# Moving the second attention projection of one group, and splitting the LayerNorm of its two tiles, in a fused attention + MLP kernel

## The chip, the cores and the metric

The kernel runs on one core of one Trainium2 chip. A core has a matrix engine (PE, with PEld for its weight loads), a vector engine (DVE), a scalar engine (ACT), a general engine (POOL), a queue engine that only issues transfers (SP), and 16 DMA engines. Each engine works through its own instructions in the order in which the program lists them, and waits when one of them needs something that is not there yet. The metric is the device time of one execution in microseconds (us), lower is better.

## What is computed

A pre-norm transformer block on 2048 tokens of width 576, in bfloat16:

```
h  = x + Attention(LayerNorm(x), wqkv) @ wo        # 32 heads of 18
       # token s attends to tokens s, s-2, s-4, ... s-14  (8 keys, softmax)
h2 = h + gelu(LayerNorm(h) @ w1 + b1) @ w2 + b2    # inner width 4608
```

## The kernel before

**Tiles.** The tokens are cut into 16 tiles of 128; tile j holds tokens j, j+16, j+32 and so on, one per partition. So the 8 keys of a tile's tokens lie in tiles of the same parity, and two rings in SBUF (`kv_ring`, one for even tiles and one for odd ones, 8 slots each for keys and values) hold all that a tile needs. Where the window wraps around, the slot must hold the tile shifted down by one partition: `store_halo` writes a tile's keys and values to DRAM, and `halo(j, 1)` (keys) or `halo(j, 2)` (values) reads them back shifted, as soon as the tile itself has been used.

**Stages.** First come the LayerNorm of x and the products with `wqkv` (about 5 to 69 us of the profile). Then the tiles go in pairs, `GROUPS[0]` to `GROUPS[7]`: (14, 12), (10, 8), (6, 4), (2, 0), (15, 13), ... For each pair k a loop body emits MLP1 (`h @ w1` and gelu, 36 row blocks of 128) and MLP2 (`@ w2`). Groups 0 and 1 do MLP2 with 36 rows of matmuls per tile (`mlp2`, line 576); groups 2 to 7 use `mlp2_fast` (line 661), a scheme that needs fewer products of 2x2 blocks but wants sums and differences of the weights (`w2_sums`, line 631) and of the activations (`h_sums`, line 641) from DVE.

**What is threaded between the matmuls.** While group k is in its MLP, the other engines prepare the groups behind it. In the loop body, c and d are the two tiles of group k+1, and e and f those of group k+2. In the round k = 0 that this document is most about, c = 10, d = 8, e = 6, f = 4.

- Attention of a tile, on DVE: `att_qk_a` (line 345, keys times query), `att_qk_rest` (lines 351, 358, 360, then the maximum, 364 and 365), then `att_exp` on ACT (line 383), then `att_den` (391 to 393) and `att_pv_a`, `att_pv_b` (397, 403, 404), which leave the output of attention in `q_all`.
- Its transposition: `dma_out` writes it to a DRAM buffer `td` (lines 193, 194) and a transposing DMA reads it back as `oT` (line 199 or 433), all from SP.
- Projection with `wo`, on PE: `wo_visit` or `wo_duo` (line 217, tile `pw`).
- LayerNorm 2: `ln2_h` (DVE, 461) adds x; `ln2_act` (ACT, 478 to 480) takes mean and variance; POOL raises the variance to the power -1/2 (481); `ln2_send` (ACT, 486 and 177) normalises and sends the tile to `td`; `ln2_ins` has the transposing DMAs that read it back as `hnT` (496), the right operand of MLP1, and two accumulating DMAs from POOL (505) behind them. Both halves of `hnT` are needed before MLP1 of that group begins. `put_b2` (SP, 502) overwrites the tile's x with the bias b2.

**What sets the order.** The order is written by hand: the whole kernel stands in a block in which every engine keeps the program's order. The lists `m1[v]` run ahead of visit v of MLP1 (four visits), `mid[v]` between its phases, and `ia[f]` and `ib[f]` ahead of row f of MLP2 of the group's first and second tile. `late_wo` is a projection that is slipped into the last visit of MLP1. A `wo_visit` with `fill=True` runs two rows of MLP2 between its two halves. ACT changes between two function tables, one with exp and one with gelu; `exps` is an exp followed by `gelu_table`, a one-element gelu that brings the second table back. `after` and `between` are the lists of the qkv stage, by visit: `after[n]` runs behind visit n, `between[n]` behind the first output of visit n.

Of the kernel before, what the change touches and what calls it, by code (L numbers as in the profile page):

```python
# [17 lines left out]
def kernel(  # L18
# [12 lines left out]
    nc = tc.nc  # L31
# [71 lines left out]
    def load(out, in_):  # L103
        ins = nc.sync.dma_start(out=out, in_=in_).ins
        if pace[0] is not None:
            tc.add_manual_dep(ins, pace[0].name, sync_dep, reason="pace of the weight loads")

    def load_x(js):
        j0, n, step = js[0], len(js), 2
        load(x_all[:, j0:j0 + step * (n - 1) + 1:step, :], x3[:, j0:j0 + step * (n - 1) + 1:step, :])  # L110

    def load_wqkv(t, k0=0, k1=KF):
        load(wq_sb[:, k0:k1, t * D:(t + 1) * D],
             A_wqkv[k0 * P:k1 * P, t * D:(t + 1) * D].rearrange("(k p) c -> p k c", p=P))

    def load_wqkv_half(engines, ts):
        src = A_wqkv[KF * P:D, :].rearrange("p (t g c) -> p t g c", t=3, g=2)
        for r in range(2):
            engines[r].dma_start(out=wqh_sb[half_rows(r), ts, :], in_=src[:, ts, r, :])
# [87 lines left out]
    def half_rows(r):  # L207
        return slice(r * HP, (r + 1) * HP)
# [121 lines left out]
    def logit_of(js):  # L330
        home, i = side[js[0]]
        return (x_all[:, 13:16:2, 0:2 * W * H].bitcast(F32).rearrange("p i (w h) -> p i w h", w=W)
                if home else logits[:])[:, i:i + len(js)]

    def sides(js):
        i = side[js[0]][1]
        return slice(i, i + len(js))

    def halo(j, t):
        if j >= 2:  # L340
            ring = (None, k_ring, v_ring)[t]
            nc.sync.dma_start(out=ring[j % 2][:, j // 2, :], in_=kv_dram[j, 0:P, t - 1, :])
# [46 lines left out]
    def att_den(*js):  # L389
        n, sl, lg = len(js), sides(js), logit_of(js)  # L390
        nc.vector.tensor_reduce(out=den[:, sl], in_=lg.rearrange("p i w h -> p i h w"), axis=AX.X, op=ALU.add)  # L391
        nc.vector.reciprocal(out=den[:, sl], in_=den[:, sl])
        nc.vector.tensor_tensor(out=probs[:, sl], in0=lg, in1=den[:, sl].unsqueeze(2).to_broadcast([P, n, W, H]), op=ALU.mult)
# [12 lines left out]
    def att_pv_sum(j):  # L406
        att_pv_a(j)
        att_pv_b(j)
# [264 lines left out]
    def c_(fn, *a):  # L673
        return lambda: fn(*a)
# [71 lines left out]
    with tc.manual_schedule(engines={ENG.PE, ENG.Activation, ENG.DVE, ENG.SP, ENG.Pool}):  # L746
# [1 line left out]
        load_x(EVEN[1:2])  # L748
        load_wqkv(1, 0, 2)
        load_wqkv(1, 2, KF)  # L750
        load_wqkv_half((nc.scalar, nc.scalar), slice(1, 3))
        load_x(EVEN[2:3])
        load_x(EVEN[3:4])
        load_wqkv(2, 0, 2)
        load_wqkv(2, 2, KF)
        load_x(EVEN[4:6])
        load_x(EVEN[6:8])
        load_x(ODD[0:4])
# [75 lines left out]
        A = ATT_ORDER  # L834
# [15 lines left out]
        def ln2_stats(c, d):  # L850
            for j in (c, d):
                ln2_h(j)
                ln2_act(j)
            for j in (c, d):
                put_b2(j)
# [5 lines left out]
                for j in (c, d):  # L861
                    accumulate_h(j)

        def ln2_pair(c, d, js=()):
            ln2_stats(c, d)
            if js:
                att_den(*js)
                att_pv_sum(js[0])
            ln2_send(c)
            ln2_send(d)  # L870
            ln2_ins(c, d)
            if js:
                halo(js[0], 2)

        loads = {v: [c_(load_w1, c)] for c, v in enumerate((3, 4, 9, 14, 16, 18))}
        for n, v in enumerate((20, 21, 22, 23)):
# [3 lines left out]
            1: [c_(ln1_even_rstd, 2, 3), c_(ln1_even, 5)],  # L880
            2: [c_(ln1_even, 6), c_(ln1_even, 7), c_(ln1_even_rstd, 4, 5)],
            3: [c_(ln1_even_rstd, 6, 7), c_(ln1_stats, 8)],
            4: [c_(ln1_rstd, 8), c_(ln1_stats, 9, c_(ln1_bias, 8)), c_(ln1_act, 8, 0), c_(ln1_stats, 10)],
            5: [c_(ln1_act, 8, 1), c_(out_x, 0), c_(ln1_rstd, 9), c_(ln1_bias, 9), c_(att_qk_a, A[0])],
            6: [c_(ln1_rstd, 10), c_(ln1_act, 8, 2), c_(halo, A[0], 1)],
            7: [c_(att_qk_rest, A[0], 0), c_(ln1_bias, 10), c_(ln1_act, 8, 3), c_(in_x, 0), c_(out_x, 1)],
# [12 lines left out]
            20: [c_(ln2_rstd, A[1]), c_(add_b2, A[1]), c_(ln2_bias, A[1]), c_(att_qk_rest, A[2], 0, 1)],  # L899
        }  # L900
        between = {
            10: [c_(att_exp, A[0])],
            13: [c_(att_exp, A[1])],
            18: {1: [c_(tr_o, A[1], "D")]},
# [55 lines left out]
        def wo_visit(*duos, fill=False):  # L960
            visit([wo_duo(j, tag) for j, tag in duos], (lambda: [ahead[0]() for _ in range(2)]) if fill else None)
# [5 lines left out]
        for k, g in enumerate(GROUPS):  # L967
            c, d = GROUPS[k + 1] if k + 1 < len(GROUPS) else (None, None)
            e, f = GROUPS[k + 2] if k + 2 < len(GROUPS) else (None, None)
            m1, mid, ia, ib, late_wo = {0: []}, {}, {}, {}, None  # L970
            if k in (1, 2):
                m1[0].append(c_(finish_out, GROUPS[k - 1][1]))
            if k == 0:
                m1[0] += [c_(halos, 1), c_(att_qk_a, d), c_(att_qk_rest, d, 1), c_(halo, d, 1)]
                mid[0] = {1: [c_(exps, d)]}
                m1[1] = [c_(pv_t, c), c_(pv_t, d), c_(load_w2, 4), c_(att_qk, e, 0)]
                late_wo = wo_duo(c, "B")
                ia[12] = [c_(exps, e), lambda d=d: wo_visit((d, "A"), fill=True), c_(ln2_pair, c, d, (e,)), c_(halos, 2), c_(send_o, e)]
                ib[0] = [c_(finish_out, g[0])]
                ib[4] = [c_(att_qk, f, 1)]  # L980
                ib[8] = [c_(read_o, e)]
                ib[32] = [c_(exps, f)]
            elif k == 1:
                m1[0].append(c_(pv_t, d))
                m1[1] = [c_(att_qk_a, e), c_(halo, e, 1), c_(att_qk_b, e, 0), c_(halos, 7)]
                m1[3] = [c_(att_qk_a, f), c_(halo, f, 1), c_(att_qk_add, f, ((0, 0, 9), (0, 0, 4)))]
                ia[0] = [c_(wo_visit, (c, "B"), (d, "C")), c_(ln2_pair, c, d), c_(att_qk_b, f, 1, 2), c_(att_max, (e, f)),
                         c_(exps, e, f), c_(att_qk_one, GROUPS[4][0], 0, 1), c_(att_den, e, f)]
                ia[2] = [c_(pv_sum, e), c_(dma_tr_o, e), c_(reload_x, GROUPS[4])]
                ib[0] = [c_(finish_out, g[0])]  # L990
            if k < 2:
                mlp1(g, mlp1_plan(p, q, r, s, (s, r, p) if k else (r, s, p)), m1, mid, late_wo)
                mlp2_tile(g, 0, "D", ia)
                mlp2_tile(g, 1, "C", ib)
                continue
            rows = ROWS[k]
            home = k % 2
            x = {n: [] for n in ("h", "6", "7", "in", "exp", "4", "3")}
            if k < 6:
                m1[0] += [c_(pv_sum, d), c_(send_o, d), c_(read_o, d)]  # L1000
                m1[1] = [c_(att_qk_one, f, 1, home ^ 1), c_(att_max, (e, f))]
                m1[3] = []
                if k in (2, 3):
                    m1[3] += [c_(w2_sums, *((0, 8) if k == 2 else (8, 12)))]
                early = {2: (), 3: (0,)}.get(k, (0, 2))
                m1[3] += [c_(h_sums, 0, rows, early)]
                x["h"] += [c_(h_sums, 0, rows, [t for t in range(4) if t not in early])]
                x["exp"] += [c_(exps, e, f), c_(att_den, e, f)]
                x["4"] += [c_(att_pv_a, e), c_(halo, e, 2)]
                x["3"] += [c_(att_pv_b, e), c_(send_o, e), c_(read_o, e)]  # L1010
            else:
                if k == 6:
                    m1[0] += [c_(pv_sum, d), c_(send_o, d), c_(read_o, d)]
                    m1[1] = [c_(w2_sums, *m) for m in ((12, 14), (14, 16), (16, NM))]
                m1[3] = [c_(h_sums, 0, SR)]
                mid[3] = {1: [c_(h_sums, SR, 16)]}
                x["h"] += [c_(h_sums, 16, NM)]
            if k + 3 < len(GROUPS):
                x["7"] += [c_(att_qk_one, GROUPS[k + 3][0], 0, home)]
                x["in"] += [c_(reload_x, GROUPS[k + 3])]  # L1020
            wo = None
            if c is not None:
                if k == 6:
                    x["h"] = [c_(ln2_h, c), c_(ln2_act, c), c_(ln2_h, d)] + x["h"] \
                        + [c_(ln2_more, d), c_(ln2_rstd, d), c_(ln2_send, c), c_(add_b2, c), c_(add_b2, d), c_(ln2_bias, d)]
                    x["6"] += [c_(ln2_hn, d), c_(ln2_out, d)]
                else:
                    x["h"] = [c_(ln2_stats, c, d)] + x["h"]
                    x["6"] += [c_(ln2_send, c)]
                    x["7"] = [c_(ln2_send, d)] + x["7"]  # L1030
                x["in"] = [c_(ln2_ins, c, d)] + x["in"]
                wo = lambda tags: wo_visit((c, tags[0]), (d, tags[1]))
            mlp1(g, mlp1_plan(p, q, r, s, (r, s, p)), m1, mid)
            mlp2_fast(g, rows, (p, q, r, s), wo, x)
            p, q, r, s = r, s, p, q
# [30 lines left out]
```

## Time and profile before

| | us |
|---|---|
| median of 6 runs | 368.08 (367.01 to 369.2) |
| the profiled execution | 368.53 |
| its span, first to last instruction | 366.6 |
| PE busy / DVE busy / ACT busy / POOL busy in the span | 358.7 / 299.7 / 231.8 / 40.9 |
| qkv stage ends, MLP1 of group 0 begins | about 69 |
| MLP2 of group 0 begins | 87.6 |
| MLP1 of group 1 begins | 108.1 |
| MLP2 of group 1 begins | 128.1 |
| MLP1 / MLP2 of group 2 begin | 145.8 / 163.6 |
| MLP1 / MLP2 of group 3 begin | 184.2 / 202.0 |

The profile is of one execution, and all moments in it count from the first instruction. A row of a timeline gives the start, the time, the engine, the source line, the operation, the output and inputs, how many instructions are merged in the row, and in brackets the idle time ahead of it with what ended it. A row of the waits gives who waited, for what, the total, how often, and the longest. In rows of SP the time is that of issuing; a transfer lands later. The granted clock of PE was 0.999 of the full one over the span.

### The profile page before, as it was taken

To read this page: it belongs to the slowest core of one execution; us is meant where nothing else is said; L and a number is where in the kernel's file an instruction comes from. 1 tells how busy PE (TensorE), PEld (TensorE's weight loads), DVE (VectorE), ACT (ScalarE), POOL (GpSimd) and SP (SyncE) were. 2 spreads that over 40 slices of the span, in tenths; PEclk is the share of its full clock that TensorE was granted. 3 is DMA by queue.
4 is the path that set the end of the run, shared out by engine and by line. 5 is a ranking of instruction groups with operands and counts; after the bars stand their busy time and mean duration, and the time that the engine had idled before them with its cause. 6 is when DMAs were issued, how large, how long until landed. Compare 5 with 4: busy or idle time off the path is not lost.

```text
span 366.6 us, 11432 instructions
## 1 busy us (share of the span) xinstructions
PE 358.7 (98%) x4899; PEld 292.4 (80%) x4899; DVE 299.7 (82%) x425; ACT 231.8 (63%) x511; POOL 40.9 (11%) x47
## 2 busy tenths in 40 slices
PE   8999999998999999998999999999999999999995
PEld 4689877887778877886788778877887788778874
DVE  4899999999999799999989998999994599720331
ACT  4788856798638754666646774686468656616620
POOL 2242004000220032001110021011101100100000
PEclk9999999999999999999999999999999999999999
DMA  7997798952558533630453136304520442030001
GB/s 244 318 272 228 173 209 237 320 196 70 178 153 154 198 114 75 113 87 34 114 115 82 35 89 131 89 32 109 120 66 33 89 85 55 3 89 18 2 2 33
DMA packets 61875, 43.70 MB, mean 119 GB/s; under 512 B 31856, under 2 KB 60144, under 8 KB 61824
## 3 DMA queue, kind: packets, MB, share of 16 engines
q1 hardware_dynamic: 59808, 41.05, 40.3%
q0 software_dynamic: 1728, 1.77, 4.7%
q8 instruction: 38, 0.62, 0.7%
q10 hardware_dynamic: 288, 0.15, 0.2%
q14 instruction: 13, 0.11, 0.1%
HBM read 21.10 MB, written 12.42 MB: 91 GB/s over the span
## 4 chain that ended last, share of the span: by engine, by line
PE 52%; DVE 6%; DMA 2%; ACT 1%; issue 1%; DVEq 0%
PE po L661 25%; PE pm L217 24%; PE pw L217 3%; DVE prod L397 1%; DMA kv_ring<-kv_dram 1%; DVE prod L351 1%; DVE prod L345 1%; DVE prod L403 1%; DMA x_all<-b_bc 1%; DVE q_all L631 0%; DVE x_all L631 0%; DVE w2a_sb L631 0%; ACT L383 0%; DVE den L391 0%; DVE peak L364 0%
## 5 line engine op out<-in xcount | busy, mean ns | idle before, releaser
L557 ACT ACTIVATE h_all<-pm,b_sb 128x256 f16<-128x256 f32 (+1 forms) x288 | 108.5, 497 | 67.2 <-PE pm L217 67.2
L217 PE MATMUL pm<-hnT,w_sb 64*128 64x256 bf16 x2304 | 143.0, 269 | 0.0
L217 PEld LDWEIGHTS <-w_sb 64*128 64x128 bf16 x2304 | 111.8, 94 | 15.0 <-issue 1.7
L661 PEld LDWEIGHTS <-h_all 128*128 128x128 f16 x544 | 52.3, 98 | 15.3 <-issue 2.5
L217 PE MATMUL pq<-wq_sb,xnT 64*128 64x288 bf16 x768 | 54.6, 283 | 0.8 <-DMA wq_sb<-in_A_wqkv_dram 0.6
L217 PEld LDWEIGHTS <-xnT 64*128 64x128 bf16 x864 | 43.8, 94 | 9.9 <-issue 1.1
L351 DVE TENSOR_TENSOR prod<-prod 128x2304 bf16<-128x2304 bf16 (+1 forms) x64 | 44.2, 691 | 2.1
L397 DVE TENSOR_TENSOR prod<-kv_ring,probs 128x4608 bf16<-128x4608 bf16 x16 | 40.9, 2555 | 3.5 <-DMA kv_ring<-kv_dram 3.2
L661 PE MATMUL po<-w2a_sb,h_all 128*128 128x288 bf16 (+1 forms) x312 | 43.6, 286 | 0.0
L345 DVE TENSOR_TENSOR prod<-kv_ring,q_all 128x4608 bf16<-128x4608 bf16 x16 | 40.9, 2553 | 2.2 <-DMA kv_ring<-kv_dram 2.0
L217 PE MATMUL pm<-hnT,w1h_sb 64*128 64x256 bf16 x288 | 39.2, 269 | 0.0
L481 POOL TENSOR_TENSOR ln_rstd<-ln_var,mhalf 128x1 f32<-128x1 f32 x13 | 15.9, 1220 | 184.0 <-ACT ln_var L480 184.0
L403 DVE TENSOR_TENSOR prod<-prod 128x2304 bf16<-128x2304 bf16 (+1 forms) x32 | 33.8, 1057 | 1.0
L576 PEld LDWEIGHTS <-h_all 128*128 128x128 bf16 x288 | 27.9, 98 | 7.9 <-issue 1.0
L661 PEld LDWEIGHTS <-kv_ring 128*128 128x128 f16 x240 | 23.3, 98 | 7.5 <-DVE kv_ring L641 1.3
L576 PE MATMUL po<-w2a_sb,h_all 128*128 128x288 bf16 x224 | 28.5, 286 | 0.0
L661 PE MATMUL po<-w2b_sb,h_all 128*128 128x288 bf16 (+1 forms) x152 | 22.2, 286 | 0.0
L217 PE MATMUL pw<-wo_sb,oT 64*128 64x288 bf16 x256 | 19.5, 283 | 1.1 <-DMA oT<-td 1.1
L641 DVE TENSOR_TENSOR kv_ring<-h_all 128x1536 f16<-128x1536 f16 (+3 forms) x10 | 6.9, 685 | 16.0 <-ACT h_all L557 16.0
L164 POOL TENSOR_TENSOR ln_rstd<-ln_veps,mhalf 128x1 f32<-128x1 f32 (+2 forms) x14 | 13.5, 972 | 49.1 <-DVE ln_veps L158 34.1
L217 PEld LDWEIGHTS <-oT 64*128 64x128 bf16 x288 | 13.5, 94 | 6.0 <-DMA oT<-td 1.4
L505 POOL DMA_DIRECT2D x_all<-h x12 | 10.9, 1057 | 45.6 <-DMA hnT<-td 15.7
(107 smaller groups left out, 377.6 us busy)
## 6 DMA issues: line engine op xcount, KB each, us to landing
w_sb<-in_B_w_dram SPq DMA_DIRECT2D x6, 768.0 KB, 5.4
kv_ring<-kv_dram SPq DMA_DIRECT2D x28, 144.0 KB, 3.1
w2a_sb<-in_B_w_dram SPq DMA_DIRECT2D x4, 1008.0 KB, 7.3
kv_dram<-kv_ring SPq DMA_DIRECT2D x13, 288.0 KB, 3.5
out_dram<-o_sb SPq DMA_DIRECT2D x15, 144.0 KB, 2.5
td<-q_all SPq DMA_DIRECT2D x14, 144.0 KB, 2.0
td<-hn SPq DMA_DIRECT2D x14, 144.0 KB, 1.8
x_all<-in_A_x_dram SPq DMA_DIRECT2D x12, 144.0 KB, 2.8
```

The costliest lines, as they stand in the source:

```text
L164: nc.gpsimd.tensor_tensor(out=rstd[:], in0=veps[:], in1=mhalf[:].to_broadcast([P, n]), op=ALU.pow)
L217: last = nc.tensor.matmul(duo["g"][r ^ swap][i], lhsT=lhsT, rhs=rhs, start=(swap == 0 and i == 0 and kt == 0), stop=(swap == 1 and kt == K ...
L345: nc.vector.tensor_tensor(out=prod[:], in0=k_ring[j % 2], in1=q_all[:, j, :].unsqueeze(1) .to_broadcast([P, W, D]), op=ALU.mult)
L351: nc.vector.tensor_tensor(out=prod[:, :, o * H:o * H + n], in0=prod[:, :, a * H:a * H + n], in1=prod[:, :, c * H:c * H + n], op=ALU.add)
L397: nc.vector.tensor_tensor(out=prod[:].rearrange("p w (d h) -> p w d h", h=H), in0=v_ring[j % 2].rearrange("p w (d h) -> p w d h", h=H), in ...
L403: nc.vector.tensor_tensor(out=prod[:, 0:n, :], in0=prod[:, 0:n, :], in1=prod[:, n:2 * n, :], op=ALU.add)
L481: nc.gpsimd.tensor_tensor(out=rstd[:], in0=var[:], in1=mhalf[:], op=ALU.pow)
L505: ins = nc.gpsimd.dma_start(out=x_of(j), in_=h_of.pop(j)[:], accum_op=ALU.add).ins
L557: pace[0] = nc.scalar.activation(out=hT(grp)[:, f, 0:N], in_=ps[:, r, i * N:(i + 1) * N], func=ACT.Gelu_apprx_tanh, bias=b1_sb[:, f:f + 1] ...
L576: nc.tensor.matmul(banks[half], lhsT=hT(grp)[:, f, i * P:(i + 1) * P], rhs=w2_rows(f)[:, half * HALF:(half + 1) * HALF], start=(f == 0), s ...
L641: nc.vector.tensor_tensor(out=s_slot(t, m0, m1), in0=a, in1=b, op=alu)
L661: nc.tensor.matmul(bank, lhsT=l, rhs=r, start=start, stop=stop, skip_group_check=True)
```

## The change

Five edits:

1. At the start, the last 64 rows of the V weights no longer come with those of K in the two transfers that ACT issues (72 KB each, now 36 KB each); SP issues them (2 transfers of 36 KB) behind the rest of the V weights and ahead of six tiles' loads of x and more.
2. In the qkv stage, ACT normalises the first odd tile (`ln1_act(8, 0)`) behind the first output of visit 5 and no longer ahead of it.
3. In round k = 0, LayerNorm 2 of tile c comes first and alone, ahead of row 0 of MLP2: its `ln2_h` stands between `att_qk_a` and `att_qk_rest` of tile e on DVE, and its `ln2_act` and `ln2_send` stand ahead of the exp of tile e on ACT.
4. The projection of tile d moves from ahead of row 12 of MLP2 to ahead of row 19; LayerNorm 2 of d, the exp, `att_den` and PV of tile e move with it. The transposing reads of c and d stay together, behind the sending of d.
5. In round k = 3, the weight sums of row pairs 8 to 11 (four DVE instructions) move from the end of MLP1 to its beginning, ahead of PV of the second tile of group 4.

```
-        load_wqkv_half((nc.scalar, nc.scalar), slice(1, 3))
+        load_wqkv_half((nc.scalar, nc.scalar), slice(1, 2))
         load_x(EVEN[2:3])
         load_x(EVEN[3:4])
         load_wqkv(2, 0, 2)
         load_wqkv(2, 2, KF)
+        load_wqkv_half((nc.sync, nc.sync), slice(2, 3))
         load_x(EVEN[4:6])
...
-        def ln2_pair(c, d, js=()):
+        def ln2_pair(c, d):
             ln2_stats(c, d)
-            if js:
-                att_den(*js)
-                att_pv_sum(js[0])
             ln2_send(c)
             ln2_send(d)
             ln2_ins(c, d)
-            if js:
-                halo(js[0], 2)
...
-            4: [c_(ln1_rstd, 8), c_(ln1_stats, 9, c_(ln1_bias, 8)), c_(ln1_act, 8, 0), c_(ln1_stats, 10)],
+            4: [c_(ln1_rstd, 8), c_(ln1_stats, 9, c_(ln1_bias, 8)), c_(ln1_stats, 10)],
...
         between = {
+            5: [c_(ln1_act, 8, 0)],
...
             if k == 0:
...
-                m1[1] = [c_(pv_t, c), c_(pv_t, d), c_(load_w2, 4), c_(att_qk, e, 0)]
+                m1[1] = [c_(pv_t, c), c_(pv_t, d), c_(load_w2, 4), c_(att_qk_a, e), c_(halo, e, 1)]
                 late_wo = wo_duo(c, "B")
-                ia[12] = [c_(exps, e), lambda d=d: wo_visit((d, "A"), fill=True), c_(ln2_pair, c, d, (e,)), c_(halos, 2), c_(send_o, e)]
+                ia[0] = [c_(ln2_h, c), c_(ln2_act, c), c_(put_b2, c), c_(ln2_send, c), c_(att_qk_rest, e, 0)]
+                ia[19] = [c_(exps, e), lambda d=d: wo_visit((d, "A"), fill=True), c_(ln2_h, d), c_(ln2_act, d), c_(put_b2, d),
+                          c_(att_pv, e), c_(ln2_send, d), c_(ln2_ins, c, d), c_(halo, e, 2), c_(halos, 2), c_(send_o, e)]
...
             if k < 6:
+                if k == 3:
+                    m1[0] += [c_(w2_sums, 8, 12)]
                 m1[0] += [c_(pv_sum, d), c_(send_o, d), c_(read_o, d)]
                 m1[1] = [c_(att_qk_one, f, 1, home ^ 1), c_(att_max, (e, f))]
                 m1[3] = []
-                if k in (2, 3):
-                    m1[3] += [c_(w2_sums, *((0, 8) if k == 2 else (8, 12)))]
+                if k == 2:
+                    m1[3] += [c_(w2_sums, 0, 8)]
```

## The prediction

> **What bounds the kernel now.** I read the busy shares first.
>
> ```profile
> PE 358.7 (98%) x4899; PEld 292.4 (80%) x4899; DVE 299.7 (82%) x425; ACT 231.8 (63%) x511; POOL 40.9 (11%) x47
> ```
>
> PE is busy almost throughout, so a change that leaves PE's work alone, as this one does, can only win the few places where PE waits. The waits of PE between 80 and 180 us show two:
>
> ```profile
> PE pw L217 <- DMA oT<-td: 1.1, 1, 1.1
> PE po L661 <- DVE kv_ring L641: 1.0, 1, 1.0
> ```
>
> The timeline of PE places them:
>
> ```profile
> 91.84 0.66 PE L217 MATMUL pw<-wo_sb,oT 64*128 64x288 bf16 x8 [1.14 <-DMA oT<-td]
> ...
> 171.56 1.16 PE L661 MATMUL po<-q_all,kv_ring 128*128 128x288 f16 x8 [0.96 <-DVE kv_ring L641]
> ```
>
> The first is the projection that the change moves. The second, in MLP2 of group 2, waits for DVE, so I asked what DVE did before it: its waits from 63.5 to 172 us.
>
> ```profile
> DVE prod L345 <- DMA kv_ring<-kv_dram: 2.0, 1, 2.0
> DVE prod L397 <- DMA kv_ring<-kv_dram: 0.4, 1, 0.4
> DVE den L391 <- ACT logits L383: 0.2, 1, 0.2
> ```
>
> That is all: 2.7 us of idleness in 108 us, and none from 63.5 to 123.6. The chain that ended last says the same: before 171 us it runs through DVE, behind 173.8 through PE alone.
>
> ```profile
> 150.41 2.57 DVE prod L397
> ...
> 168.85 0.68 DVE h L461
> ...
> 173.80 10.45 PE po L661 x84
> 184.25 17.79 PE pm L217 x324
> ```
>
> So up to 171.5 us DVE is the bound and PE has 0.96 us to spare; from there on PE is. **Time that PE wins before 171.5 us comes back as a longer wait there. Time that DVE loses after 63.5 us is lost at the end.** The change removes no DVE work before 171.5 us.
>
> **The projection of tile 8 (edit 4).** `oT` is issued at 89.12 and lands 2.7 later (the tile's view), 91.8. PE could have begun at 91.84 - 1.14 = 90.7. Seven rows are 14 matmuls; 24 of them take 87.58 to about 90.5, 0.123 each, so 1.72. PE comes at 92.4, finds `oT` there for 0.6, and the 1.14 go. Next late is `hnT`: MLP1 of group 1 begins at 108.07, and the second transposing read, issued at 105.15, lands 2.7 to 2.8 later (107.9). PE, 1.14 earlier, would want it at 106.9.
>
> **The exp of tile 6 (edits 3 and 4).** This is the costly part. ACT before:
>
> ```profile
> 89.35 1.28 ACT L383 ACT_TABLE_LOAD   x1
> 94.30 0.42 ACT L383 ACTIVATE logits<-logits 128x256 f32<-128x256 f32 x1 [3.67 <-DVE logits L365]
> 94.74 1.28 ACT L533 ACT_TABLE_LOAD   x1
> 96.03 0.20 ACT L533 ACTIVATE warm<-mhalf 128x1 f32<-128x1 f32 x1
> 96.14 0.67 ACT L478 ACTIVATE hn<-h 128x576 bf16<-128x576 f32 x1
> ```
>
> The exp table was loaded under DVE's QK, and the exp ran beside the two `h` additions (94.19 to 95.6), so `att_den` began at 95.52 without idleness. Now ACT does LN2 of tile 10 first:
>
> - DVE ends `att_qk_a` at 89.58; `h` of tile 10 ends near 90.25 and puts 0.67 (distance of the two L461 rows) into the queue. The logits are ready at 94.27 + 0.6 = 94.9, `h` of tile 8 ends at 95.5.
> - ACT begins L478 at 90.3. L478 to L480 took 1.99 (96.14 to 98.13): 92.3. POOL begins 0.15 later.
> - POOL's power depends on DVE:
>
> ```profile
> 98.28 1.66 POOL L481 TENSOR_TENSOR ln_rstd<-ln_var,mhalf 128x1 f32<-128x1 f32 x1 [34.99 <-ACT ln_var L480]
> ...
> 133.16 0.56 POOL L481 TENSOR_TENSOR ln_rstd<-ln_var,mhalf 128x1 f32<-128x1 f32 x1 [22.73 <-ACT ln_var L480]
> 135.05 2.75 POOL L481 TENSOR_TENSOR ln_rstd<-ln_var,mhalf 128x1 f32<-128x1 f32 x1 [1.33 <-ACT ln_var L480]
> ```
>
>  Beside a reduction it takes 0.56; beside a long product of DVE it ends 0.4 after that product (99.94 after 99.53; 137.80 after 137.40). Here DVE runs additions of 0.29 to 0.69: 0.6 to 0.9, to 93.2. Bounds: 0.56, and 2.75.
> - L486 and L177 took 1.20 (99.97 to 101.17): 94.4. The table load, on the path now, 1.28: 95.7. The exp, 0.42: 96.1.
>
> `att_den` begins at 96.1 to 96.4 and not at 95.52: **DVE idles, +0.6 to +0.9; I take 0.7.** By POOL's bounds it is +0.5 to +2.7.
>
> The Trainium skill, "ScalarE: Activation LUTs", section "What ACT_TABLE_LOAD costs", speaks against this edit more strongly: a switch costs the load of about 1.28 us and a drain of about 1.38 more. By that the exp would be 1.4 us later still, and the forecast 370.3. The trace shows the load alone: loaded at 94.74 in 1.28, the next activation stands at 96.03. I go by the trace.
>
> **LN2 of tile 8.** Behind the exp come the gelu table and warm-up, about 1.5 (94.74 to 96.23), so L478 of tile 8 begins near 97.7, where it began at 98.03 before. Its power waits for the end of PV's product (0.4 after 100.1, so 100.6), L486 and L177 end at 101.8, before 102.56. SP has the reads of both tiles behind the sending of tile 8, as before, and `hnT` lands some 0.7 earlier, at 107.2. PE keeps 0.7 of its 1.14. The sending of tile 10 stands early on SP, where nothing else is queued that could run.
>
> **What follows the late `att_den`.** PV of tile 6, `finish_out`, QK and the exp of tile 4, PV of tile 4 and QK of tile 2 are back to back on DVE to 123.6, all 0.7 later. The 2.00 idle that follows is no cushion: the keys' read that ends it is issued from SP behind `att_pv` of tile 4, its sending (117.39) and the transposing read (119.96), which move with DVE. LN2 of group 2 starts from DVE (130.22), so it moves too. The late gelus of group 1 (from 111.95, now 112.7) cost nothing: the first bank is wanted again two visits (7.9) after 107.3, at 115.2, and is empty at about 114.3. The second wait of PE grows to 0.96 + 0.7 + what PE has won, and the end moves by what DVE has lost.
>
> **The start (edits 1 and 2).** Not shown in the trace; bounds for DVE, whose first work waits for x (2.6 in two waits): 72 KB less ahead of x, at 318 GB/s of that slice 0.2 earlier; two more issues on SP ahead of the later x, their kind took 0.59 and 1.21 there, and 0.4 of transfer: up to 0.4 later. I take +0.1. Edit 2 ends a PE wait of 0.2 on L312, before 63.5 and not on DVE: nothing at the end.
>
> **The weight sums (edit 5).** Four instructions, 202.67 to 205.67, 3.0. At 188.0 DVE idles 1.56 for a values' read, and they fit there; PV of tile 13 is 1.45 later, so its `oT` lands near 201.1, and PE wants it at 203.6. PE does not wait there before or after: 0. If the cover were gone, the projection has 2.4 to lose first.
>
> **Sum:** +0.7 + 0.1 = +0.8. On the profiled execution (368.53 around a span of 366.6) that is 369.3 and 367.4; it stands 0.45 over the median of 368.08, from which I forecast 368.9.
>
> **Rivals.**
> - *A, the forecast:* DVE late by 0.5 to 1.4, 368.5 to 369.5. Chance 0.55.
> - *B, nothing is lost:* the exp is in time because POOL and the first-tile work are quicker than their rows, or the 2.00 idle absorbs the delay. For it: this idle is longer than 0.7. Against: its transfer is issued behind DVE's own result. 368.1 +- 0.5. Chance 0.15.
> - *C, faster:* that same keys' read takes 4.35 from issue to landing (121.26 to 125.6), where the one issued at 106.46 took 2.45. If its length is chance traffic and the shift takes it out, DVE wins 1.9, less 0.8: -1.1, 367.0. It decides once the read lands over 0.8 sooner after its issue. Against: seven stores of 288 KB follow it in both kernels. Chance 0.12.
> - *D, dearer:* POOL's power falls beside a long product (2.75 and not 0.7), or ACT's late gelus hold up PE in group 1: +1.5 to +2.9, 369.6 to 371. Against: only short additions stand there. Chance 0.18.
>
> **Numbers.** A measurement of this kernel can tell about 0.3% (1.1 us) from no change. Faster (below 367.0): C, 0.12. Slower (above 369.2): D and a quarter of A, 0.32. Within: 0.56. The range runs from B's lower end to the middle of D, 367.6 to 370.2, and leaves out C and the rest of D.
>
> **What would show it.** After: the wait for `oT` gone and PE waiting a little for `hnT` ahead of MLP1 of group 1; a new idle of 0.6 to 0.9 on DVE ahead of L391 by the exp, behind the first table load; the DVE wait of PE at L661 in group 2 above 2 us; no PE wait in group 3. I am wrong if DVE reaches the `h_sums` of group 2 no later than 170.1, or if PE's last wait is elsewhere.

## The result, and the profile after

| | before | after |
|---|---|---|
| median, us | 367.43 (366.8 to 369.78, 72 runs) | 367.47 (366.62 to 370.69, 35 runs) |
| profiled execution / span | 368.53 / 366.6 | 367.49 / 365.7 |
| end of PE's last product | 362.79 | 362.34 |

The ratio after/before is 1.0001, 95% interval 0.9992 to 1.0009: no change that can be measured. The forecast (368.9) was too high by 1.4, and the time fell just below the range (from 367.6). Part of that is the base: the six runs that the forecast started from had a median of 368.08, the 72 one of 367.43. And the profiled execution of before, from which all durations were read, was 1.1 above that median; this will turn out to matter. A profile is always of one execution, so each reading below holds for that one until another profile has it too.

The busy shares of after, from its page:

```profile
PE 359.4 (98%) x4899; PEld 293.5 (80%) x4899; DVE 299.6 (82%) x425; ACT 231.9 (63%) x511; POOL 39.7 (11%) x47
```

They hardly differ from before's, so the waits must tell. The waits of PE over the whole span of after (who waited for what: total, how often, longest):

```profile
PE po L661 <- DVE kv_ring L641: 0.9, 1, 0.9
PE busy L771 <- PEq L1051: 0.8, 1, 0.8
PE po L576 <- DMA w2b_sb<-in_B_w_dram: 0.5, 1, 0.5
PE pq L217 <- ACT kv_ring L312: 0.3, 1, 0.3
PE pq L217 <- DMA wq_sb<-in_A_wqkv_dram: 0.2, 1, 0.2
```

The `oT` wait of 1.14 is gone, and PE does not wait for `hnT`. A wait for `w2b_sb` is new. The wait at L661, which was to grow above 2, stands at 0.9. The timeline of PE in after places the two:

```profile
92.44 0.67 PE L217 MATMUL pw<-wo_sb,oT 64*128 64x288 bf16 x8
...
94.36 1.89 PE L576 MATMUL po<-w2a_sb,h_all 128*128 128x288 bf16 x14
96.72 0.53 PE L576 MATMUL po<-w2b_sb,h_all 128*128 128x288 bf16 x3 [0.47 <-DMA w2b_sb<-in_B_w_dram]
...
171.11 1.15 PE L661 MATMUL po<-q_all,kv_ring 128*128 128x288 f16 x8 [0.95 <-DVE kv_ring L641]
```

`w2b_sb` holds rows 28 to 35 of `w2`, 1.18 MB, issued by SP right behind the transposing read of tile 8. It lands 6.4 us later, at 96.7. Before, PE began row 28 at 97.19; now it comes at 96.25 and finds the load under way. So the next late transfer stood 4 us behind the projection, and not at 107.

DVE in after, from 63.5 to 172 us, has two waits longer than 0.55. First its waits in that stretch, then the two rows of its timeline:

```profile
DVE prod L345 <- DMA kv_ring<-kv_dram: 1.5, 1, 1.5
DVE den L391 <- ACT logits L383: 0.9, 2, 0.6
```

```profile
96.02 0.58 DVE L391 TENSOR_REDUCE den<-logits 128x32 f32<-128x256 f32 x1 [0.61 <-ACT logits L383]
...
125.61 2.56 DVE L345 TENSOR_TENSOR prod<-kv_ring,q_all 128x4608 bf16<-128x4608 bf16 x1 [1.49 <-DMA kv_ring<-kv_dram]
```

The new idle ahead of `att_den` is there, 0.61, and ACT's rows ahead of it are the forecast ones (times forecast: L177 done 94.4, exp 95.7 to 96.1). `att_den` itself is 0.50 later than the 95.52 of before, less than its idle, because `h` of tile 8 ended 0.1 earlier.

```profile
93.39 0.87 ACT L177 ACTIVATE hn<-h,ln_nmean,ln_rstd 128x576 bf16<-128x576 f32 x1
94.28 1.28 ACT L383 ACT_TABLE_LOAD   x1
95.57 0.42 ACT L383 ACTIVATE logits<-logits 128x256 f32<-128x256 f32 x1
```

But the idle ahead of the QK of tile 0, called "no cushion", shrank from 2.00 to 1.49, and that product starts at 125.61, where it was 125.63. DVE is 0.50 late from 96.0 up to 120.5 (every row of its timeline) and on time from 125.6 on. Near 150 it comes to stand 0.48 earlier than before: the wait of 0.43 for a values' read that stands in before's list is not in after's. The same product, in before and in after:

```profile
150.41 2.56 DVE L397 TENSOR_TENSOR prod<-kv_ring,probs 128x4608 bf16<-128x4608 bf16 x1 [0.43 <-DMA kv_ring<-kv_dram]
```

```profile
149.93 2.56 DVE L397 TENSOR_TENSOR prod<-kv_ring,probs 128x4608 bf16<-128x4608 bf16 x1
```

So DVE reaches the sums of group 2 (`h_sums`) at 169.65, where it was 170.10. That is the prediction's own sign of being wrong (no later than 170.1):

```profile
169.65 0.68 DVE L641 TENSOR_TENSOR kv_ring<-h_all 128x1024 f16<-128x1024 f16 x1
```

The chain that ended last shows PE alone behind 173.34, where it was 173.80:

```profile
168.40 0.68 DVE h L461
...
173.34 10.45 PE po L661 x84
183.79 17.79 PE pm L217 x324
```

So the profiled execution ended 0.45 earlier on PE, by what DVE gained near 150 (another 0.47 of span lies behind the last product and DVE's last row, where the program has nothing that differs). The medians say that even this is not the rule.

### The profile page after: what moved, and what is told of

It is laid out like the page before. It is cut to its first block, busy times and chain, and to the rows that moved or that the text cites. A ratio compares the mean times of both kernels' runs of the same rounds, so it can differ in the third digit from the quotient of the medians.

```text
span 365.7 us, 11434 instructions
## 1 busy us (share of the span) xinstructions
PE 359.4 (98%) x4899; PEld 293.5 (80%) x4899; DVE 299.6 (82%) x425; ACT 231.9 (63%) x511; POOL 39.7 (11%) x47
## 4 chain that ended last, share of the span: by engine, by line
PE 52%; DVE 7%; ACT 1%; issue 1%; DMA 1%; DVEq 0%
PE po L661 25%; PE pm L217 24%; PE pw L217 3%; DVE prod L397 1%; DVE prod L403 1%; DVE prod L351 1%; DVE prod L345 1%; DMA x_all<-b_bc 1%; DVE o_sb L738 0%; DVE q_all L631 0%; DVE x_all L631 0%; DVE w2a_sb L631 0%; ACT L383 0%; DVE peak L364 0%; DVE den L391 0%
## 5 line engine op out<-in xcount | busy, mean ns | idle before, releaser
L217 PE MATMUL pm<-hnT,w_sb 64*128 64x256 bf16 x2304 | 143.1, 269 | 0.0
L217 PEld LDWEIGHTS <-w_sb 64*128 64x128 bf16 x2304 | 113.1, 94 | 13.7 <-issue 1.7
L661 PEld LDWEIGHTS <-h_all 128*128 128x128 f16 x544 | 52.3, 98 | 15.3 <-issue 2.5
L217 PE MATMUL pq<-wq_sb,xnT 64*128 64x288 bf16 x768 | 54.5, 283 | 0.5 <-ACT kv_ring L312 0.3
L217 PEld LDWEIGHTS <-xnT 64*128 64x128 bf16 x864 | 43.0, 94 | 10.4 <-issue 0.9
L661 PE MATMUL po<-w2a_sb,h_all 128*128 128x288 bf16 (+1 forms) x312 | 43.6, 286 | 0.0
L217 PE MATMUL pm<-hnT,w1h_sb 64*128 64x256 bf16 x288 | 39.4, 269 | 0.0
L576 PEld LDWEIGHTS <-h_all 128*128 128x128 bf16 x288 | 27.8, 98 | 8.5 <-issue 1.6
L481 POOL TENSOR_TENSOR ln_rstd<-ln_var,mhalf 128x1 f32<-128x1 f32 x13 | 14.6, 1122 | 183.3 <-ACT ln_var L480 183.3
L661 PEld LDWEIGHTS <-kv_ring 128*128 128x128 f16 x240 | 23.4, 98 | 7.4 <-DVE kv_ring L641 1.3
L576 PE MATMUL po<-w2a_sb,h_all 128*128 128x288 bf16 x224 | 28.5, 286 | 0.0
L661 PE MATMUL po<-w2b_sb,h_all 128*128 128x288 bf16 (+1 forms) x152 | 22.2, 286 | 0.0
L641 DVE TENSOR_TENSOR kv_ring<-h_all 128x1536 f16<-128x1536 f16 (+3 forms) x10 | 6.9, 686 | 16.0 <-ACT h_all L557 16.0
L217 PE MATMUL pw<-wo_sb,oT 64*128 64x288 bf16 x256 | 19.5, 283 | 0.0
L217 PEld LDWEIGHTS <-oT 64*128 64x128 bf16 x288 | 13.5, 94 | 4.8 <-issue 1.7
L730 ACT COPY po<-po 128x288 f32<-128x288 f32 x18 | 6.9, 385 | 14.6 <-PE po L661 11.4
```

The source lines that it names most:

```text
L217: last = nc.tensor.matmul(duo["g"][r ^ swap][i], lhsT=lhsT, rhs=rhs, start=(swap == 0 and i == 0 and kt == 0), stop=(swap == 1 and kt == K ...
L481: nc.gpsimd.tensor_tensor(out=rstd[:], in0=var[:], in1=mhalf[:], op=ALU.pow)
L576: nc.tensor.matmul(banks[half], lhsT=hT(grp)[:, f, i * P:(i + 1) * P], rhs=w2_rows(f)[:, half * HALF:(half + 1) * HALF], start=(f == 0), s ...
L641: nc.vector.tensor_tensor(out=s_slot(t, m0, m1), in0=a, in1=b, op=alu)
L661: nc.tensor.matmul(bank, lhsT=l, rhs=r, start=start, stop=stop, skip_group_check=True)
L730: nc.scalar.copy(out=bank[seed[step][1]], in_=bank[seed[step][0]])
```

## Experiments

Ratios stand against the kernel before on the same chip, with 95% intervals; the experiments ran on four chips, so medians are compared only on one chip, unless it is said otherwise. Where an edit added lines to the kernel, its line numbers are up to 4 higher (L578 is L576, L219 is L217, L645 is L641). "Keys' read" is always the shifted read of the keys of tile 2 in MLP1 of group 1 (SP, L342, near 121 us), for which the QK of tile 0 waits; some expectations call it that of group 2. Its length is from issue to landing. "Sums" are the `h_sums` of group 2 that PE needs at L661.

**Is DVE really the bound up to 171 us?** If so, 1.28 us more on DVE cost 1.28, wherever they stand between 63.5 and 171. Two kernels add to before one extra product (the first half of a QK product, written again at once, so nothing else changes): e2 near 103 us, ahead of the keys' read, e3 near 135 us, behind it.

```
-                ib[4] = [c_(att_qk, f, 1)]
+                ib[4] = [c_(att_qk_half, f), c_(att_qk, f, 1)]                       # e2
...
-                         c_(exps, e, f), c_(att_qk_one, GROUPS[4][0], 0, 1), ...
+                         c_(exps, e, f), c_(att_qk_half, GROUPS[4][0]), c_(att_qk_one, ...   # e3
```

> The kernel before, and DVE does half of the product of QK of tile 4 once more ahead of it (1.28 us, same values) in MLP2 of group 0, near 103 us, ahead of the DVE wait of 2.0 us for a keys' read. Theory of the prediction (the keys' read is issued behind DVE's own work, so the wait moves and is no cushion): the wait of 2.0 stays, 1.28 us slower than before. Rival 1 (the traffic of the transfers around 108 to 120 us gives this read a floor in time, which takes up about 0.5, as in the changed kernel): the wait is 1.5, and the wait of 0.43 at 150 us goes too: 0.4 to 0.8 us slower. Rival 2 (a full cushion): the wait falls to 0.7 and the time stays.

> The kernel before, and DVE does half of the product of QK of tile 15 once more ahead of it (1.28 us, same values), near 135 us, behind the DVE wait of 2.0 us. Theory (DVE is the bound from there to 171.5): 1.28 us slower, or 0.85 if the wait of 0.43 at 150 us takes up a part. Rival (PE sets the end): no change, as PE has no work of its own that this delays.

e2: 1.0025 [1.0013, 1.0037], about 0.9. e3: 1.0008 [0.9993, 1.0023], about 0.3. **In both profiles PE's wait at L661 of group 2 is gone**, although DVE has more to do. DVE's second sum and PE's first product that needs it, in e3:

```profile
169.06 0.69 DVE L645 TENSOR_TENSOR kv_ring<-kv_ring,h_all 128x1024 f16<-128x1024 f16 x1
```

```profile
170.44 1.14 PE L665 MATMUL po<-q_all,kv_ring 128*128 128x288 f16 x8
```

The sum is done at 169.75, 0.7 before PE comes, with 1.28 more on DVE than in before. In these executions PE is the bound. My theory (1.28, or 0.85 at the least) falls for e3. In e3's profile DVE waits nowhere for the keys' read, which took 2.65 and not 4.35. In e2 the sum was done only 0.06 before PE came, with a read of 3.25, and that profile is of the fastest of its 12 executions (367.71). So DVE may well be late in the others, which would explain why e2 loses more than e3; no profile of a slower one shows it.

**Edit 4 without the split of LN2** (the whole list at row 19; on before):

```
-                ia[12] = [c_(exps, e), lambda d=d: wo_visit((d, "A"), fill=True), c_(ln2_pair, c, d, (e,)), ...
+                ia[19] = [c_(exps, e), lambda d=d: wo_visit((d, "A"), fill=True), c_(ln2_pair, c, d, (e,)), ...
```

> The kernel before, with its whole list of row 12 (exp of tile 6, projection of tile 8, LayerNorm 2 of both tiles) called ahead of row 19: on DVE, ACT, POOL and SP nothing changes its place, only PE does 14 more matmuls ahead of the projection. Theory (DVE sets the moment 171.5 us, and what PE wins before it comes back as a longer wait there): the wait of 1.14 us for oT goes, the wait of PE for h_sums in group 2 grows from 0.96 to about 2 us, or to 1.5 if a load of w2 takes part of it as in the changed kernel (0.5), and the time is that of before within 0.2 us. Rival (PE sets the end throughout): 1.1 us faster than before, with the wait in group 2 unchanged.

1.0011 [0.9996, 1.0026]. PE no longer waits for `oT` and waits 1.9 for `w2b_sb` instead; the wait at L661 that the theory let grow isn't there. This profile is of the slowest of its 12 executions (370.02), in which the load took 7.6 (5.9 in before). In it, what the projection's move wins, the weight load takes.

**The order of the keys' read.** In e4 (on before) and e5 (on after), SP issues this read ahead of the transposing read of tile 4 and not behind it (the expectation of e5 speaks of an instruction fetch; "What makes the read long" explains it):

```
-                m1[0].append(c_(pv_t, d))
-                m1[1] = [c_(att_qk_a, e), c_(halo, e, 1), c_(att_qk_b, e, 0), c_(halos, 7)]
+                m1[0] += [c_(pv, d), c_(send_o, d)]
+                m1[1] = [c_(att_qk_a, e), c_(halo, e, 1), c_(read_o, d), c_(att_qk_b, e, 0), c_(halos, 7)]
```

> The kernel before, and on SP in MLP1 of group 1 the read of the shifted keys of tile 6's successor in the ring, which DVE waits for, is issued ahead of the transposing read of tile 8's successor and no longer behind it: issued near 120.0 and not at 121.26. Theory (DVE up to 171.5 is the bound and this wait of 2.0 is in its chain): the wait falls to 0.7 to 0.9, h_sums in group 2 come 1.1 to 1.3 earlier, of which the kernel keeps what PE waits there (0.96, and 0.1 for the second copy): 0.9 to 1.1 us faster. If the read only lands as late as before because of traffic: no change. Rival (DVE's chain does not set the end): no change though the wait falls.

> The kernel after, with SP's order in group 1 changed as in e4: the shifted keys' read of group 2 is issued ahead of the transposing read and not behind it. Theory (the keys' read of 4.38 us in the trace after, 121.21 to 125.59, is stretched by the instruction fetch that starts at 122.2 and takes 2.06): issued nearly 1 us sooner the read lands before or early in the fetch, takes 2.2 to 3.2, the DVE wait for it (1.49) falls to 0.5 or less, PE's wait at L661 in group 2 (0.9) goes, and the end comes 0.7 to 1.0 sooner: about 366.6 against 367.5 of the kernel before. Rival 1 (the read is long because of what the other queues move, stores and weight loads): it stays over 4 us, the wait at L661 stays at 0.5 or more, the time is within 0.3 of after. Rival 2 (DVE is late by its own work, the 0.6 ahead of the denominator): the keys' wait falls but L661 still waits 0.6 or more.

e4: 0.9999 [0.9985, 1.0013], where 0.9 to 1.1 us less was expected; its read took 2.14, DVE doesn't wait for it, and PE doesn't wait at L661. The 2.00 of DVE's idle and the 0.96 at L661 could thus be removed from before without a gain that can be measured; the second profile of before, below, has 0.9 of the one and nothing of the other. e5: 0.9983 [0.9969, 0.9996], 367.06 against 367.59, less than the 0.7 to 1.0 expected. The read took 2.15. PE's waits and timeline in e5:

```profile
PE po L576 <- DMA w2b_sb<-in_B_w_dram: 0.8, 1, 0.8
```

```profile
169.76 1.14 PE L661 MATMUL po<-w2b_sb,h_all 128*128 128x288 bf16 x8
170.74 1.14 PE L661 MATMUL po<-q_all,kv_ring 128*128 128x288 f16 x8
```

At 170.74 there is no wait; DVE had the sums done at 169.9, 0.8 earlier. So in the changed kernel the keys' read seems to cost about 0.6 by the ratios (1.0001 for after, 0.9983 for e5), and in before nothing that can be measured. The intervals of after and e5 overlap a little; a pair on one chip, e15 and e16 below, differs in this order alone and settles it better.

**The same kernels profiled again.** These two show what belongs to one execution and what to the kernel.

> The kernel before, unchanged, profiled a second time. Theory (the long keys' read of the first profile, 4.35, and the 2.00 idle of DVE behind it belong to that execution, in which an instruction fetch of 1.86 fell into the read): this profile shows the read at 2.1 to 3.3 when no fetch starts within 2 us of its issue, else 2.3 and the fetch's length together; without a fetch no wait of PE at L661 in group 2, oT 1.1 to 1.5. Rival (the read's length belongs to the kernel): 4.3 again, DVE idle of 2.0, PE wait at L661 of 1.0.

> The kernel after, unchanged, profiled a second time. Theory: DVE's idle ahead of L391 stays at 0.6 and PE's wait for w2b_sb at 0.5 to 0.8, since these belong to the kernel; the keys' read takes 2.3 plus the length of the fetch that falls into it, if one does, and PE's wait at L661 follows it (0.9 at 4.4, none below 3.5). Rival: all as in the first profile, 4.4 and 0.9.

Before, second profile (367.90), waits of PE, then of DVE from 63.5 to 172 us:

```profile
PE pw L217 <- DMA oT<-td: 1.4, 1, 1.4
```

```profile
DVE prod L345 <- DMA kv_ring<-kv_dram: 0.9, 1, 0.9
```

The wait at L661 of group 2, on which my bound rested, isn't there; the `oT` wait is. The profiles of e17 and e18 below, which keep before's order, don't have it either. After, second profile (368.53):

```profile
PE po L576 <- DMA w2b_sb<-in_B_w_dram: 1.2, 1, 1.2
PE po L661 <- DVE kv_ring L641: 1.0, 1, 1.0
```

```profile
DVE prod L345 <- DMA kv_ring<-kv_dram: 1.5, 1, 1.5
```

DVE's idle of 0.6 ahead of L391 is there again. The keys' read took 3.79 in the first and 4.38 in the second, so before is not free of long reads either. Both lengths missed their expectations: 2.1 to 3.3 in before, as no fetch began within 2 us of the read's issue, and 3.85 in after (2.3 and a fetch of 1.55). PE's wait for `w2b_sb`, 1.2, was longer than the 0.5 to 0.8 expected.

**What makes the read long.** The page lists a queue that moves next to nothing:

```profile
q8 instruction: 38, 0.62, 0.7%
```

By name and number these are fetches of PE's instructions: 38 packets of 16 KB, one about every 7 us in MLP1. PE has 4899 products and 4899 weight loads, 258 of them to a packet. A packet takes 0.9 to 2.1 us, where the data packets around it take 0.04 in the mean. From the packets of every trace of this study:

```
keys' read     took  part of an instruction fetch within it
after          4.38  2.06      (again: 4.38, 1.55)
before         4.35  1.86      (again: 3.79, 0.52)
e8             3.86  1.45
e6             3.56  0.95
e15            3.38  1.25
e16            3.26  1.15
e2             3.25  1.18
e18            3.10  0.45
e17            2.81  0
e3             2.65  0.33
e1             2.63  0
e14            2.61  0
e7             2.53  0.50
e5             2.15  0.41
e4             2.14  0
e12            2.10  0.06
```

With 0.95 or more of a fetch inside, all eight reads took 3.25 to 4.38, that of e15 among them, though it is issued first there as in e5. Of the ten with 0.52 or less, eight took 2.10 to 2.81, two 3.10 and 3.79 (in the 3.79 one data packet took 1.3 ahead of the fetch; why, stays open). The place on SP counts too: with 0.5 or less of a fetch inside, the reads issued first (e4, e5, e7, e12) took 2.1 to 2.5, those behind the transposing read (e1, e3, e14, e17, e18) 2.6 to 3.1. To move the fetches and nothing else, PE's warm-up, whose columns count for nothing, was cut into more instructions: 48 more in e8, 144 more in e14.

```
-        for n in [512] * 8 + [P] * 5:
+        for n in [P] * 37:               # e8
+        for n in [56] * 84 + [32]:       # e14
```

> The kernel after, with the warm-up of PE ahead of the work cut into more and shorter products: 37 of 128 columns in place of 8 of 512 and 5 of 128, the same columns in all, 48 more instructions of PE. The fetches of PE's instructions, one after every 256 instructions, so stand 24 products earlier in the program (about 2.3 to 3 us in MLP1). Theory: the fetch that starts at 122.2 in the trace after starts near 119.5 and is over before the keys' read is under way: that read falls from 4.38 to 3 or less, the DVE wait for it from 1.49 to 0.3 or less, PE's 0.9 at L661 goes, and the time is 0.7 to 0.9 under after, 366.7. Rival (traffic of the stores and loads, or DVE's own lateness): the read and the wait at L661 stay as they are, within 0.3 of after.

> The kernel after with PE's warm-up cut into 85 products (84 of 56 columns, one of 32: the same columns) in place of 13, 144 more instructions of PE, so that every fetch stands 144 instructions (72 products) earlier in the program: near 118.2 and 125.3 instead of 122.2, with the keys' read at 121.2 between them (e8, with 48, moved it by 1.3 only). Theory: the read takes 2.2 to 2.7, DVE waits 0.3 or less for it, PE does not wait at L661 of group 2. The time says less, since the fetches of the first 70 us are moved too, and the reads of xnT there can be hit or missed: 366.5 to 368.5. Rival (the read is long because of the stores or of its place behind the transposing read): it stays over 4, with DVE's 1.5.

In e8 the fetch moved by 24 products, 1.3 us of MLP1 (324 products in 17.79), and with the rest of the kernel 2 us later it fell on the read again: 3.86. That expectation failed by a wrong step of mine: I had put 24 products at over 2 us. Also, a fetch of 1.76 fell on a transposing read of `xnT`, which took 5.86 (3.78 in after), and PE waited there. Time 1.0011 [0.9993, 1.0029]. In e14 the fetch came at 119.66, ahead of the read. The read took 2.61, and PE doesn't wait at L661. The queue of SP in e14, and the same moments in after:

```profile
119.25 0.43 SPq L194 DMA_DIRECT2D td<-q_all  x1
122.10 1.21 SPq L199 DMA_TRANSPOSE oT<-td  x1
123.40 0.53 SPq L342 DMA_DIRECT2D kv_ring<-kv_dram  x1
```

```profile
119.90 1.21 SPq L199 DMA_TRANSPOSE oT<-td  x1
121.21 0.53 SPq L342 DMA_DIRECT2D kv_ring<-kv_dram  x1
```

Now the fetch fell on the sending of tile 4 ahead of it: 2.96 from issue to landing where after has 1.78, and SP stood waiting for it until 122.10. DVE still waits 0.9, where 0.3 or less was expected. So in these traces transfers that met a fetch mostly took longer, in the pairs compared here by up to 2.1 us, but not every one and not by the same: a sending in e1 with 0.9 of a fetch inside took only 0.4 more, and the transposing read of tile 4 in after, which a fetch met in its last 0.5, took its usual 2.8. All 18 traces from 70 us on agree: the stores of the output took 1.76 in the median without a fetch inside (166 of them) and 4.34 with 0.9 us or more of one (72), though other traffic may differ between these places too. e14's time, 1.0034 [1.0018, 1.0050], is worse; only part of it shows in its profile (PE stands 0.9 later at 27 us), so it says nothing for or against the fetch.

**What the late weight load takes.** e6 and e7 (with the keys first) issue `w2b_sb` ahead of the values' reads, on after; e12 splits it in two transfers at its old place, on e5.

```
-                m1[1] = [c_(pv_t, c), c_(pv_t, d), c_(load_w2, 4), c_(att_qk_a, e), c_(halo, e, 1)]
+                m1[1] = [c_(load_w2, 4), c_(pv_t, c), c_(pv_t, d), c_(att_qk_a, e), c_(halo, e, 1)]   # e6, e7
...
-        load(dst, B_w2[f0 * P:f1 * P, :].rearrange("(ft p) c -> p ft c", p=P))
+        parts = ((f0, f1),) if c < 4 else ((f0, f0 + 5), (f0 + 5, f1))                                # e12
+        for a0, a1 in parts:
+            load(dst[:, a0 - f0:a1 - f0, :], B_w2[a0 * P:a1 * P, :].rearrange("(ft p) c -> p ft c", p=P))
```

> The kernel after, with the load of the second half of w2 (w2b_sb, first used in row 28 of MLP2 of tile 10) issued on SP ahead of the values' loads in MLP1 of group 0 and not behind them. Theory (DVE and the keys' read set the moment 171.5, PE the rest): PE's wait of 0.5 for w2b_sb goes, but the 0.5 comes back in the wait at L661 of group 2, which grows from 0.9 to 1.4: no change from after, within 0.3 us, as long as the keys' read is stretched. Rival (PE is the bound all along, and the wait at L661 is chance in the profiled execution): 0.5 sooner, 367.0.

> Both edits of the two kernels ahead of it: keys' read first on SP, second half of w2 loaded earlier. Theory: PE waits neither for oT, nor for w2b_sb, nor at L661: 1.14 + 0.5 - 0.3 less of waits than after, PE waits below 0.6 us in all, about 366.1 to 366.6, that is 0.9 to 1.4 under the kernel before. Rival (both gains are taken by a wait that is not seen yet, of DVE at L661 or for hnT ahead of MLP1 of group 1 at 107.4): within 0.4 of 367.4.

> After, with the keys' read first (e5) and the second half of w2 loaded by two transfers at its old place, rows 28 to 32 and rows 33 to 35. Theory (PE reaches row 28 before the one transfer of 6.4 to 6.6 has landed, but needs its rows one by one, 0.25 each): the wait of 0.5 to 0.8 for w2b_sb falls to 0.2 or less; the next late is hnT, which landed 0.25 to 0.5 ahead of PE's first product of group 1, so PE keeps 0.2 to 0.5 of it: 366.5 to 366.9. Rival (DVE decides again, at L661): no change from e5, 367.1.

All three missed. e6: 1.0040 [1.0020, 1.0061], slower, and e7: 1.0017 [1.0001, 1.0033]. The load, issued at 75.53, lands at 83.32, and the values' read queued behind it took 5.62 instead of 2.14. In e6, DVE then waits 1.7 for it, and PE for the `oT` that follows (in e7 too, 1.4; and in both PE waits another 0.7 to 0.8 ahead of MLP1 of group 1):

```profile
87.33 0.66 PE L217 MATMUL pw<-wo_sb,oT 64*128 64x288 bf16 x8 [1.13 <-DMA oT<-td]
```

e12: 0.9982 [0.9969, 0.9995], as e5. The first five rows came in time, the other three landed at 98.9, later than the one transfer in e5 (97.45):

```profile
96.56 1.39 PE L578 MATMUL po<-w2b_sb,h_all 128*128 128x288 bf16 x10
98.96 0.90 PE L578 MATMUL po<-w2b_sb,h_all 128*128 128x288 bf16 x6 [1.01 <-DMA w2b_sb<-in_B_w_dram]
```

So the load was halved without moving anything: e15 on e5, e16 on after, e17 on before as control. These three kernels leave out rows 32 to 35 of `w2` and use rows 28 to 31 twice, so they don't compute the block; they serve to time the load alone.

```
-        return w2a_sb[:, f, :] if f < FA else w2b_sb[:, f - FA, :]
+        return w2a_sb[:, f, :] if f < FA else w2b_sb[:, (f - FA) % 4, :]
...
+        f0 += 4 * (m0 >= 16)                                 # the same for the weight sums
...
+        f1 -= 4 * (c == 4)
+        dst = dst[:, 0:4, :] if c == 4 else dst
         load(dst, B_w2[f0 * P:f1 * P, :].rearrange("(ft p) c -> p ft c", p=P))
```

> The keys-first version of after (e5) with only half of the late weight load: rows 28 to 31 of w2 are loaded, and MLP2 uses them a second time in place of rows 32 to 35, which are left out. 0.59 MB in place of 1.18. Theory (in after and in e5 PE gives back 0.5 to 1.2 us of what it wins at oT in the wait for this load, and nothing else is late before 173): the load lands near 93.5 to 94, PE's wait of 0.8 in row 28 goes, hnT (0.25 to 0.5 ahead of PE) is next and takes up to half of it back: 366.4 to 366.8, 0.3 to 0.6 under e5. Rival (DVE decides at L661 of group 2 or hnT lands later than PE wants it by as much): as e5, 367.1.

> The kernel after with the same half load (rows 32 to 35 of w2 left out, rows 28 to 31 used twice). Theory (in after the keys' read of group 2 sets DVE, and DVE sets 171): PE's wait for w2b_sb of 0.5 to 1.2 goes and comes back at L661 of group 2, 0.9 to 1.0 now, 1.4 to 2 then: 367.2 to 367.6, no change from after. Rival (PE is the bound all along): 366.6 to 367.0.

> The kernel before with the same half load, a control for the lighter traffic (rows 32 to 35 of w2 left out, rows 28 to 31 used twice). PE never waits for this load in before: theory no change, 367.2 to 367.9; oT wait still 1.1 to 1.5. Rival (the load slows other transfers that count, the reads around 90 to 98): 0.4 or more sooner.

| | ratio | PE's waits from 85 to 175 us |
|---|---|---|
| e17 (before, half) | 0.9993 [0.9983, 1.0004] | `oT` 1.4 |
| e16 (after, half) | 0.9984 [0.9972, 0.9996] | `hnT` 0.4 |
| e5 (after, keys first) | 0.9983 [0.9969, 0.9996] | `w2b_sb` 0.8 |
| e15 (after, keys first, half) | 0.9964 [0.9950, 0.9978] | `hnT` 0.2 |

Three of these ran on one chip, e5 on another. The lighter load alone is worth nothing that can be measured to before. To the changed kernel it is worth about 0.6 by the ratio, but its median, 367.27, is only 0.2 under that of e17 (367.47), so alone its worth isn't clear of the control. Together with the keys' read it is worth 1.3 by the ratio (366.51, 1.0 under e17): about as much as PE waits for `oT` in before, no longer given back. e15 and e16 differ in the keys' read alone, and e15 is 0.76 sooner. What stays open: before with both the half load and the keys' read first was not run, so that these two are worth nothing without the move is shown for each alone, not for both. And with the load out of the way `hnT` is the next late. PE's timeline in e15, then in e16:

```profile
105.13 2.12 PE L578 MATMUL po<-w2b_sb,h_all 128*128 128x288 bf16 x16
107.47 0.61 PE L219 MATMUL pm<-hnT,w_sb 64*128 64x256 bf16 x8 [0.22 <-DMA hnT<-td]
```

```profile
107.34 0.61 PE L219 MATMUL pm<-hnT,w_sb 64*128 64x256 bf16 x8 [0.41 <-DMA hnT<-td]
```

e16's profile has no wait at L661, where 1.4 to 2 was expected: its fetch was 1.15 and its keys' read 3.26. It is the profile of the fastest of its runs, which spread from 366.36 to 368.11; the median, 367.27, lies in the expected range. e15 and e17 came in as expected.

**Edits 1, 2 and 5 alone** (on before, with edits 3 and 4 undone; their lines stand in the diff above).

> The kernel before with the edits at the start and of the weight sums alone (1, 2 and 5): the V half rows from SP, the first odd tile's normalisation behind the first output of visit 5, the weight sums of rows 8 to 11 ahead of PV in group 4. Theory: nothing at the end, within 0.3 of before; PE's wait on ACT at L312 0.2 to 0.3 in another place; oT wait 1.1 to 1.5 as before. Rival (these edits carry a gain that edits 3 and 4 lose, or the other way): 0.4 or more off before.

0.9995 [0.9981, 1.0008]; `oT` 1.2, the ACT wait of 0.3 now at `kv_ring`. They change nothing that can be measured.

The best version whose computation is complete is e5: 367.06 against 367.59. e12, on another chip, equals it by the ratio.

## Why the prediction was wrong, step by step

- **"The 2.00 idle that follows is no cushion": the step that failed.** It said that the keys' read moves with DVE. DVE was 0.50 late at the sending of tile 4 (117.89, 117.39 before), but the sending took 1.78 and not 2.34, so the transposing read was issued at 119.90 against 119.96. In before a fetch of 0.96 that began at 116.79 had overlapped that sending; in the second profile of before, where the fetch ended ahead of it, the sending took 1.80. So the 0.56 that I took for a part of the chain was most likely a collision of one execution, and its absence paid DVE's loss. Then the read itself was long in both profiles, 4.35 and 4.38. Rival B named this outcome (the idle absorbs the delay) and had 0.15 from me; that the idle absorbed it was chance, for it took the shorter sending.
- **"Up to 171.5 us DVE is the bound and PE has 0.96 us to spare": wrong for the usual execution.** It holds in the one profiled, 1.1 above the median, and even there the 0.43 for the values' read near 150, which I had counted into DVE's chain, went away in after (0.6 in its second profile). With a shorter read DVE has 0.7 to 1.1 to spare at 171 (e3, e4, e5 and the second profile of before), extra work on it costs less than its length (e3), and PE pays for `oT` in full. Rival C's doubt ("chance traffic") was the right question about that 4.35; I gave it 0.12, and put its answer on the changed kernel instead of on the base.
- **"Next late is `hnT`": one transfer too far.** `w2b_sb` landed at 96.37 in before, 0.8 ahead of its use at 97.19 (0.6 ahead in the second profile). Of the 1.14 no more than 0.8 could be kept, and PE gave back 0.5 to 1.2. The waits list of before can't show a load that is in time by 0.8; its landing time could. With that load out of the way `hnT` landed at 107.20 in e16 (forecast 107.2) and PE waited 0.2 to 0.4.
- **The exp of tile 6: right.** Idle 0.61 (0.6 to 0.9 forecast), POOL's power 0.67, L177 done at 94.26, exp done at 95.99. Only the loss was a little less than the idle, 0.50, and 0.7 went into the sum. On the table load the trace agrees with the row that I took, against "ScalarE: Activation LUTs" of the Trainium skill, section "What ACT_TABLE_LOAD costs": load at 94.28 for 1.28, exp at 95.57, with no further 1.38.
- **The start and the weight sums: right within what can be told.** e18 is at 0.9995; +0.1 and 0 were forecast. The cover was thinner than forecast, though: the `oT` of tile 13 landed at 202.2 in after and not near 201.1, because its read took 4.5 and not 2.7, still 0.9 ahead of PE.
- **The sum.** +0.8 was DVE's loss carried to the end (0.7) and the start (0.1). What the runs put in its place: 1.1 to 1.5 won at `oT`, 0.5 to 1.2 given back at `w2b_sb`, and about 0.6 to 0.8 through DVE's lateness and the keys' read (e5 against after, e15 against e16). These are ranges from different executions; their balance lies around nothing, which is what was measured. The other 0.65 of the miss is the base.

## What to carry to other kernels

Ahead of a step that moves earlier, list the landing times of everything it will need, not only the waits that exist: a load that is in time by 0.8 us is the next wait. Ask of every long transfer on which a chain rests whether the same transfer is as long in another profile, above all when the profiled execution lies over the median. And when two edits each show no change, try them together: the keys' read was worth nothing alone on before, and 0.17% with the projection moved; with the load halved as well it was 0.36%, each within about 0.14%.

## What was not expected of the hardware

**Instruction fetches are visible in transfer times.** "Runtime: NRT & Kernel Launch" of the Trainium skill, section "Instruction fetch mechanics", says that instructions are refilled in blocks of 256 (16 KiB) through a queue of the engine's own, and that the cost is "mostly hidden". The count here agrees (38 packets for PE's 9798 instructions, and 256 to a packet would make 38.3), and in after PE shows no wait put down to them between 85 and 175 us. But one such packet took 0.9 to 2.1 us, and most transfers that met one became longer: the keys' read took 3.3 to 4.4 instead of mostly 2.1 to 2.8, a sending 2.96 instead of 1.78. Why a transfer waits for a fetch the traces don't show, only the times. Some SP issues that began beside a fetch were longer too: 2.37 for a store at 122.27 in after, where the other six of that row took 0.42 to 0.74. Instructions added early on PE moved the later fetches (48 of them by 1.3 us of MLP1 in e8), and so may move waits in stages that were not touched.
